# A short convolution and a SwiGLU block on one core: the copy that holds back the first weight transfers, and the order of the work of the first two pairs

## The chip, the core and the metric

The kernel runs on one core of one Trainium2 chip. The core has five engines with a queue of instructions each: TensorE (PE; its weight loads are listed as PEld), VectorE (DVE), ScalarE (ACT), GpSimd (POOL) and SyncE (SP), which here only issues DMAs. Each engine works through its queue in order; between engines, semaphores say when something is ready. The metric is device microseconds (us) from one launch.

## What is computed

```python
w = softmax(weight)                      # 8 heads x 7 taps
x_pad = concat(zeros(B, 6, D), x)        # x: 8 x 4096 x 192, fp32
att[b, s, h, :] = sum_k w[h, k] * x_pad[b, s + k, h, :]      # heads of 24 columns
x = att.reshape(32768, 192)
xn = x / sqrt(mean(x * x) + 1e-6) * rms_g
g, val = xn @ w_gate, xn @ w_val         # 192 -> 1536
out = (g * sigmoid(g) * val) @ w_out     # 1536 -> 192
```

The three weight matrices of the second half arrive as 64-bit floats. The kernel reads each as two 32-bit words and puts a 32-bit float together from them ("conversion"). All arithmetic is in fp32 or in a split of fp32 into three parts that TensorE multiplies at its faster fp32r rate.

## The kernel before

**Pairs.** The 32,768 tokens go in 32 pairs of 512-token halves, 1,024 tokens a pair. Pair 0 is computed plainly (`plain`, L1099 to L1117, then `outer` for the output matmuls). Pair 1 multiplies fp32 operands (L890), in a Strassen-like scheme for the output (the steps `o1` to `o7`, L945, with sums of operands `h1` to `h4` made at L972). From pair 2 on, the input products run on split operands in fp32r (L918) with weights that were split during pair 1, written to DRAM (`wd`, L781) and read back through a ring of ten slots (`ring_load`, L798). Meanwhile the convolution, the norm and the split of the next pair are prepared on DVE, ACT and POOL.

**The order is written by hand.** Scheduling is manual. Pair 0's work between the engines is the string `START` and then the list `LATER`, whose letters each advance one generator: `s` silu on ACT (L1110), `v` the product with the value on DVE (L1117), `n` the norm of pair 1, `t` its way to DRAM, and `o` and `O` the conversions of the even and the odd blocks of `w_out`. A conversion of an output block takes three steps: two integer operations on DVE (L305, L313); five on ACT (L320, L321, L324, L325, L328); then one on DVE (L330) and two on POOL (L336, L337), the last of which writes 2 of the 12 row blocks of `wo_sb`. The last block that pair 0's output matmuls need is the sixth.

For pair 1 the words of `FIRST` are run in order, each placing instructions at the tail of the queues: `pN` advances TensorE's line by N steps; `Aga.1` is ACT's silu of cell a of block 1 (L995) and `Vma.1` DVE's product (L1002), which also frees the PSUM bank of that cell for a later matmul; `Vh3.5` is one operand sum on DVE (L972); `W` is one step of the weights' splitting (DVE L765, ACT L769, DVE L771, POOL L775, ACT L777, SP L781, in that order for each of ten splits); `Gmul+` is POOL's scaling of pair 2's norm (L503); `Spl`, `Sft` and `Sld` are DMAs (pair 2's tokens away and back, and pair 3's eight head loads); `An.0+` ACT's rounding of the first split operand (L683), `Gl.0+` POOL's difference (L826), `Vd.0+` DVE's (L828), `Vl.4+` DVE's (L826); `Acv0++` is ACT's first tap of pair 3's convolution (L449); `R` starts the ring.

**The first convolution.** Pair 0's convolution (`conv_first`, L391) is shared between two engines: DVE takes taps 1, 3, 5 and 6 over eight heads into `y` (first tap L420, the others L424), ACT takes taps 0, 2 and 4 head by head (L406), and TensorE adds up ACT's products in PSUM with a unit matrix (L410), four heads a group. Of ACT's last tap, `give` heads are left to DVE (L430). Then DVE adds the two sums (L436). TensorE's `heat` matmuls (L536) run ahead of it.

**The hold.** Tokens of pair 0 are loaded first, in six DMAs: the first part of each partition's rows and then the second. The weights' DMAs stand behind them on SP. To keep them from competing with the tokens, `hold` copies three elements per partition from the tokens' last rows into the tile that the first weights are to be loaded to:

```python
def hold(t):
    nc.scalar.copy(out=t, in_=x0[:, -t.shape[1] :, 0])        # L226
```

The first weight DMA (L238) writes the same place and so waits for the copy, and the copy waits for the second part of the tokens. The copy is ACT's first instruction of the convolution; ACT's L406 stands behind it.

Of the kernel before, what the change touches and what calls it, by code (L numbers as in the profile page):

```python
# [20 lines left out]
def kernel(  # L21
# [10 lines left out]
    nc = tc.nc  # L32
# [61 lines left out]
    )  # L94
    FIRST = (
# [14 lines left out]
    )  # L110
    LINE = (
# [111 lines left out]

    def hold(t):

        nc.scalar.copy(out=t, in_=x0[:, -t.shape[1] :, 0])  # L226

    def load_in(u, q):
        cols = slice(u * NF * P, (u + 1) * NF * P)
# [27 lines left out]
    def load_out(i):  # L257


        if i < 2:  # L260
            t = outs.tile([P, T // P, D], F32, name="o_sb")
            t = t[:].rearrange("p j d -> p (j d)")
        else:
            n = PF * D * 2
            t = room[i // 2 - 1][:, (i % 2) * n : (i % 2 + 1) * n]
        t = raw["out", i] = t.bitcast(U32).rearrange("p (f d two) -> p f d two", f=PF, two=2)
        for f in range(PF):
            r = (i * PF + f) * P
            nc.sync.dma_start(out=t[:, f], in_=words(moe_w_out)[r : r + P, :, :])
# [117 lines left out]

    ys = {}

    def conv_first(mine, share, give):  # L390

        t = x_sb.pop(0)
        y = ys[0] = yp.tile([P, NJ, D], F32, name="y")
        theirs = [k for k in range(K) if k not in mine]
        two = NJ // 4
        for i, k in enumerate([theirs[0], mine[-1]] + theirs[1:]):
            xk, m = t[:, k : k + NJ, :], next(kept)
            if k in mine and not share:
                continue
            cuts = (0, share) if k in mine else (0, H // 2, H)  # L400
            if k == theirs[-1]:
                cuts = (0, H // 2, H - give)
            for lo, hi in zip(cuts, cuts[1:]):
                for h in range(lo, hi):
                    hs = slice(h * GS, (h + 1) * GS)
                    nc.scalar.mul(m[:, :, hs], xk[:, :, hs], taps[:, h, k : k + 1])  # L406
                part = slice(lo * GS, hi * GS)
                for c in range(4):
                    to = ps[c][:, 0 : two * D].rearrange("p (j d) -> p j d", d=D)
                    nc.tensor.matmul(  # L410
                        out=to[:, :, part], lhsT=unity, rhs=m[:, c * two : (c + 1) * two, part],
                        start=(i == 0 and lo == 0), stop=True, skip_group_check=True,
                    )
        for k in mine:
            xk = t[:, k : k + NJ, :]
            for h in range(share if k == mine[-1] else 0, H):
                hs = slice(h * GS, (h + 1) * GS)
                w = taps[:, h, k : k + 1]
                if k == mine[0]:
                    nc.vector.tensor_scalar(  # L420
                        out=y[:, :, hs], in0=xk[:, :, hs], scalar1=w, scalar2=None, op0=ALU.mult
                    )
                else:
                    nc.vector.scalar_tensor_tensor(  # L424
                        out=y[:, :, hs], in0=xk[:, :, hs], scalar=w, in1=y[:, :, hs],
                        op0=ALU.mult, op1=ALU.add,
                    )
        for h in range(H - give, H):
            k, hs = theirs[-1], slice(h * GS, (h + 1) * GS)
            nc.vector.scalar_tensor_tensor(  # L430
                out=y[:, :, hs], in0=t[:, k : k + NJ, hs], scalar=taps[:, h, k : k + 1],
                in1=y[:, :, hs], op0=ALU.mult, op1=ALU.add,
            )
        for c in (0, 3, 1, 2):
            at = y[:, c * two : (c + 1) * two, :].rearrange("p j d -> p (j d)")
            nc.vector.tensor_tensor(out=at, in0=ps[c][:, 0 : two * D], in1=at, op=ALU.add)  # L436
            if c % 2:
                heat(at, c)
# [723 lines left out]
    def done(it):  # L1162
# [11 lines left out]
        "ipvsicpsivpisvivcpsocvpispvscipvsipsiOvpsivipsvvpsopsvcpsvOnovoOpsonvOpsnoOvnopso"  # L1174
    )
    LATER = (
        (30, "s"), (35, "v"), (45, "v"), (47, "O"), (50, "O"), (53, "O"), (55, "n"), (60, "t"),
    )
    heat(taps[:].rearrange("p h k -> p (h k)"), 1)
    heat(unity, 14)  # L1180
# [7 lines left out]
        in1=mask[:].rearrange("p (o h) -> p o h", o=1).to_broadcast([P, K, H]), op=ALU.mult,  # L1188
    )
    nc.vector.tensor_reduce(out=tp[:], in_=own[:], axis=AX.X, op=ALU.add)  # L1190
    load_in(0, nc.sync)
    load_out(0)
    load_out(1)
    load_in(1, nc.sync)
    conv_first((1, 3, 5, 6), 0, 2)
    nc.gpsimd.memset(zeros, 0.0)
    nc.sync.dma_start(out=rg_sb[LOW, :], in_=rg)
    nc.sync.dma_start(out=rg_sb[UPP, 0 : KP - 1], in_=rg[:, 1:KP])
# [107 lines left out]
```

## Time and profile before

| | |
|---|---|
| time, median of 3 runs | 2470.25 us (2469.66 to 2471.25) |
| the profiled execution's own time | 2473.39 us |
| its span, first to last instruction | 2471.6 us |
| TensorE busy | 2452.5 us (99%) |
| VectorE busy | 2024.1 us (82%) |
| ScalarE busy | 1016.2 us (41%) |
| GpSimd busy | 833.3 us (34%) |
| granted TensorE clock | 1.0 |

A row of the timeline reads: start and duration in us, engine, line of the kernel, operation, output tile and inputs, shape, how many instructions were merged; in brackets the idle time of the engine ahead of it and what ended it. `SPq` is a DMA's issue. A row of the waits reads: engine, tile and line that waited, who was waited for, then total us, times and longest us. Ends of matmuls are modelled, so TensorE's idle time is less exact than its starts.

### The profile page before, as it was taken

What the parts mean: (1) busy time and instruction counts of PE and PEld (TensorE: products, weight loads), DVE (VectorE), ACT (ScalarE), POOL (GpSimd) and SP (SyncE); (2) the same over time, 40 slices, a digit from 0 to 9 for tenths busy, and PEclk for the clock granted to TensorE, in tenths of its full rate; (3) what the DMA queues carried; (4) which work ended last, traced back from release to release, by engine and by line L of the source; (5) the groups of instructions that cost most, each with busy time, mean ns of one, the idle gap of its engine ahead of it and who ended that gap; (6) DMA issues with size and microseconds to landing.
All of it is one profiled execution on the core that took longest, in us unless ns stands there. A gap on an engine that the chain in (4) does not pass through costs nothing.

```text
span 2471.6 us, 69198 instructions
## 1 busy us (share of the span) xinstructions
PE 2452.5 (99%) x29136; PEld 1894.3 (77%) x29136; DVE 2024.1 (82%) x2530; ACT 1016.2 (41%) x1431; POOL 833.3 (34%) x624
## 2 busy tenths in 40 slices
PE   8999999999999999999999999999999999999999
PEld 5547778887777777877777778777787787777777
DVE  8688888889888789888888787888888888888864
ACT  6443434433344434344334344333444343443332
POOL 0541343423343323334333434233433333333322
PEclk9999999999999999999999999999999999999999
DMA  7364678666677666786667776666776666876653
GB/s 152 60 207 125 175 184 211 179 171 170 164 200 195 181 165 172 176 207 181 190 158 178 179 202 186 176 168 168 199 197 187 165 172 169 203 192 188 159 161 95
DMA packets 716392, 430.55 MB, mean 174 GB/s; under 512 B 510330, under 2 KB 702386, under 8 KB 716082
## 3 DMA queue, kind: packets, MB, share of 16 engines
q1 hardware_dynamic: 712336, 425.21, 66.5%
q8 instruction: 230, 3.77, 0.7%
q10 hardware_dynamic: 3746, 0.92, 0.2%
q14 instruction: 80, 0.66, 0.1%
HBM read 366.96 MB, written 58.98 MB: 172 GB/s over the span
## 4 chain that ended last, share of the span: by engine, by line
PE 90%; DVE 3%; DMA 3%; SPq 1%; issue 1%; POOL 1%; ACT 1%; DVEq 0%; POOLq 0%; ACTq 0%
PE ps L918 55%; PE ps L945 35%; DMA xb<-xd 1%; DMA ht<-in_moe_w_val_dram 1%; DMA ring<-wd 1%; SPq L154 0%; DVE ht L972 0%; POOL part L775 0%; SPq L238 0%; DVE ht L1117 0%; DVE ht L1002 0%; DVE part L771 0%; DVE y L453 0%; DMA x<-in_x_dram 0%; DVE ps L989 0%
## 5 line engine op out<-in xcount | busy, mean ns | idle before, releaser
L918 PE MATMUL ps<-part,ring 64*128 64x512 f32 x12240 | 1422.0, 389 | 2.6 <-DMA ring<-wd 1.9
L918 PEld LDWEIGHTS ps<-part,ring 64*128 64x128 f32 x12240 | 1152.9, 184 | 257.8 <-DVE ps L989 12.5
L995 ACT ACTIVATE tt<-ps 128x512 f32<-128x512 f32 x744 | 438.9, 599 | 715.8 <-PE ps L918 661.7
L1002 DVE TENSOR_TENSOR ht<-ps,tt 128x512 f32<-128x512 f32 x744 | 498.0, 686 | 254.3 <-ACT tt L995 252.2
L945 PE MATMUL ps<-ht,wo_sb 128*32 128x384 f32 (+2 forms) x7272 | 468.3, 380 | 0.8 <-POOL wo_sb L337 0.8
L972 POOL TENSOR_TENSOR ht<-ht 128x512 f32<-128x512 f32 x180 | 272.2, 1520 | 543.9 <-PE ps L945 536.4
L945 PE MATMUL ps<-ht,x 128*32 128x256 f32 (+2 forms) x6696 | 439.1, 379 | 1.3 <-DVE ht L972 1.3
L945 PEld LDWEIGHTS ps<-ht,wo_sb 128*32 128x32 f32 x7272 | 325.1, 110 | 114.5 <-issue 14.5
L945 PEld LDWEIGHTS ps<-ht,x 128*32 128x32 f32 x6696 | 299.6, 110 | 90.9 <-DVE ht L972 1.6
L989 DVE TENSOR_TENSOR ps<-ps,tt 128x1024 f32<-128x1024 f32 x240 | 295.8, 1233 | 54.3 <-ACT tt L683 22.8
L453 DVE SCALAR_TENSOR_TENSOR y<-xh,tp,y 128x1536 f32<-128x1536 f32 x186 | 336.6, 1810 | 0.2
L683 ACT COPY ps<-ps 128x1024 f32<-128x1024 f32 (+1 forms) x151 | 134.6, 891 | 408.0 <-PE ps L918 336.5
L972 POOL TENSOR_TENSOR hs<-ht 128x512 f32<-128x512 f32 x120 | 155.0, 1292 | 262.6 <-DVE ht L1002 262.6
L683 ACT COPY tt<-ps 128x384 f32<-128x384 f32 (+1 forms) x182 | 151.7, 833 | 218.6 <-PE ps L945 154.9
L482 POOL TENSOR_SCALAR r<-r 128x8 f32<-128x8 f32 x31 | 6.1, 197 | 504.5 <-DVE r L477 504.4
L945 PE MATMUL ps<-hs,x 128*32 128x128 f32 (+2 forms) x2232 | 161.4, 379 | 0.0
L972 DVE TENSOR_TENSOR ht<-ht 128x512 f32<-128x512 f32 x192 | 135.0, 717 | 15.2 <-PE ps L945 12.6
L945 PEld LDWEIGHTS ps<-hs,x 128*32 128x32 f32 x2232 | 106.9, 110 | 29.6
L828 DVE SCALAR_TENSOR_TENSOR part<-part,xb 128x1024 fp32r<-128x1024 f32 x87 | 120.1, 1381 | 0.0
L972 DVE TENSOR_TENSOR ht<-hs,ht 128x512 f32<-128x512 f32 x156 | 109.2, 747 | 11.3 <-PE ps L945 10.7
L826 POOL TENSOR_TENSOR part<-xb,part 128x1024 fp32r<-128x1024 f32 x29 | 69.7, 2403 | 124.0 <-PE ps L918 82.1
L503 POOL TENSOR_TENSOR xh<-y,s 128x1536 f32<-128x1536 f32 x30 | 89.9, 2995 | 15.1 <-DVE s L495 8.6
(133 smaller groups left out, 1417.6 us busy)
## 6 DMA issues: line engine op xcount, KB each, us to landing
ring<-wd SPq DMA_DIRECT2D x1440, 192.0 KB
xb<-xd SPq DMA_DIRECT2D x60, 512.0 KB
xd<-xh SPq DMA_DIRECT2D x240, 96.0 KB
xh<-in_x_dram SPq DMA_DIRECT2D x192, 105.0 KB
xb<-xd SPq DMA_DIRECT2D x60, 256.0 KB
out_dram<-o_sb SPq DMA_DIRECT2D x126, 96.0 KB
out_dram<-o_sb SPq DMA_DIRECT2D x62, 128.0 KB
wd<-part SPq DMA_DIRECT2D x5, 1152.0 KB
```

The lines of the kernel that those rows point to most:

```text
L453: nc.vector.scalar_tensor_tensor(out=y, in0=xk, scalar=w, in1=y, op0=ALU.mult, op1=ALU.add)
L482: nc.gpsimd.tensor_scalar(out=r, in0=r, scalar1=s / D, scalar2=s * 1e-6, op0=ALU.mult, op1=ALU.add)
L503: e.tensor_tensor(out=yn[p].rearrange("p a t -> p t a"), in0=y, in1=ss[:].rearrange("p (t o) -> p t o", o=1).to_broadcast([P, TB, GS]), op ...
L683: nc.scalar.copy(out=dst, in_=src)
L826: e.tensor_tensor(out=split_of(g, 1).bitcast(F32R), in0=src, in1=high, op=ALU.subtract)
L828: nc.vector.scalar_tensor_tensor(out=split_of(g, 2).bitcast(F32R), in0=high, scalar=1.0 + SPLIT, in1=src, op0=ALU.mult, op1=ALU.subtract,)
L918: nc.tensor.matmul(out=self.both(j, c)[:, h, :], lhsT=left[HALF[h]], rhs=right[HALF[h]], start=(first and q == 0), stop=True, skip_group_c ...
L945: nc.tensor.matmul(out=self.acc(b)[i * Q : (i + 1) * Q, at : at + n], lhsT=left, rhs=cols, start=fresh, stop=True, skip_group_check=True, ...
L972: engine[eng].tensor_tensor(out=dst, in0=a, in1=b, op=op)
L989: nc.vector.tensor_tensor(out=self.both(j, c), in0=self.both(j, "b"), in1=s5, op=ALU.add)
L995: nc.scalar.activation(out=tt[:, t, :], in_=self.both(j, c)[:, 0, :], func=AF.Silu)
L1002: nc.vector.tensor_tensor(out=self.hv(j, "abcd".index(c)), in0=self.both(j, c)[:, 1, :], in1=tt[:, t, :], op=ALU.mult,)
```

## The change

Three things. The copy of `hold` goes from ACT to DVE; the function that issues the first weights' DMAs is called inside `conv_first`, so that the copy stands in DVE's queue behind the eight heads of its first tap. One more head of ACT's last tap stays with ACT: `give` goes from 2 to 1 and the last group has three heads instead of two. And words are moved: in `LATER` the three steps of the sixth output block's conversion come earlier; in `FIRST` one `W` and then three more go behind the products of cells a and b of pair 1's block 1, and `Acv0++` and the last DMAs of pair 3's tokens go ahead of `An.0+ An.4+ Gl.0+ Vd.0+ Vl.4+`.

```diff
 def hold(t):
-        nc.scalar.copy(out=t, in_=x0[:, -t.shape[1] :, 0])
+        nc.vector.tensor_copy(out=t, in_=x0[:, -t.shape[1] :, 0])
...
-    def conv_first(mine, share, give):
+    def conv_first(mine, share, give, then):
...
-                cuts = (0, H // 2, H - give)
+                cuts = (0, H // 2, H - give) if give else (0, H // 2, H // 2 + 2, H)
...
         for k in mine:
+            if k == mine[1]:
+                then()
...
     LATER = (
-        (30, "s"), (35, "v"), (45, "v"), (47, "O"), (50, "O"), (53, "O"), (55, "n"), (60, "t"),
+        (30, "s"), (33, "O"), (35, "v"), (37, "O"), (44, "O"), (45, "v"), (55, "n"), (60, "t"),
     )
...
-    load_in(0, nc.sync)
-    load_out(0)
-    load_out(1)
-    load_in(1, nc.sync)
-    conv_first((1, 3, 5, 6), 0, 2)
+
+    def first_loads():
+        load_in(0, nc.sync)
+        load_out(0)
+        load_out(1)
+        load_in(1, nc.sync)
+
+    conv_first((1, 3, 5, 6), 0, 1, first_loads)
...
     FIRST = (
-        "Vmc.0 W p1 Gpow+ W W W p1 W p1 Agd.0 W p1 Vmd.0 Vbc+ Vh1.0 p1 Gmul+ p1 Vh3.0 W",
-        "p1 Aga.1 W W W Vma.1 Vh2.0 p1 W W p1 Spl.0+ p1 Agb.1 Vmb.1 Spl.1+ p1 Spl.2+ W p1 Spl.3+ W",
+        "Vmc.0 W p1 Gpow+ W W W p1 W p1 Agd.0 W p1 Vmd.0 Vbc+ Vh1.0 p1 Gmul+ p1 Vh3.0",
+        "p1 Aga.1 Vma.1 p3 Agb.1 Vmb.1 W W W W Vh2.0 W W Spl.0+ Spl.1+ p1 Spl.2+ W p1 Spl.3+ W",
...
-        "p1 Vmd.5 p1 Vh1.5 p2 Ac1 Sld.3++ Vh3.5 Vh2.5 An.0+ An.4+ Gl.0+ Vd.0+ Vl.4+ p3 Sld.4++",
-        "Sld.5++ Sld.6++ Sld.7++ p1 Vh4.5 p1 Vh4.0 R Acv0++ p1 As7 p4 p2 Ac2 p1 Vcv1++ Vcv2++ Vh4.3",
+        "p1 Vmd.5 p1 Vh1.5 p2 Ac1 Sld.3++ Vh3.5 Vh2.5 Sld.4++ Sld.5++ Sld.6++",
+        "Sld.7++ Acv0++ An.0+ An.4+ Gl.0+ Vd.0+ Vl.4+ p4 Vh4.5 p1 Vh4.0 R p1 As7 p4 p2 Ac2 p1 Vcv1++ Vcv2++ Vh4.3",
```

Built, the queues differ only so. On SP, POOL and TensorE the instructions and their order are the same (TensorE's last group of L410 has 72 columns a row pair instead of 48). On DVE, the copy stands between L420 and L424 and one L430 is gone; L305 and L313 of the sixth block stand ahead of the last two L1117, and its L330 ahead of the last of them; one L765 stands behind two L1002 instead of ahead of them. On ACT, the copy is gone and one L406 is added; two L995 stand ahead of an L777 and an L769 instead of behind and between them; L449 stands ahead of two L683.

## Prediction

> **What bounds the kernel now.** I read the span by stretches first, then TensorE's waits, before and behind the microsecond at which pair 2's fp32r products begin.
>
> ```profile
> span 2471.6 us, 69198 instructions
> ...
> 31.00:97.40 66.40, 66.23 (x396) 31.67 (x396) 60.06 (x88) 42.97 (x68) 15.45 (x16) 1.00 0.37 75
> 214.03:2471.60 2257.57, 2249.26 (x27434) 1779.73 (x27432) 1850.76 (x2268) 917.34 (x1252) 767.00 (x562) 1.00 0.69 178
> ...
> PE ps L918 <- DMA ring<-wd: 1.9, 5, 0.8
> ```
>
> A row of the stretches gives its length, then busy time (and number of instructions) of TensorE, its weight loads, DVE, ACT and POOL, the granted clock, the share of the DMA engines and GB/s. Behind 214 us TensorE is busy for 2249.26 of 2257.57 us at a granted clock of 1.00, and the only wait its list shows there is for the ring. No instruction of that stretch is touched. So the change can only bring its beginning forward or push it back: by what TensorE waits for in the first 214 us, and by the time at which its work starts at all. From 31 to 97.4 us TensorE is as good as full (66.23 of 66.40), so what is left is the beginning and the three waits that the steps show. Nothing here can gain more than those few microseconds of 2471.6; that is the frame of all that follows. About 0.2% (4.9 us) is what a measurement of this kernel can tell from no change.
>
> **Step 1, the hold and the shared taps.**
>
> ```profile
> 5.03 5.30 PE L536 MATMUL ps<-part 128*128 128x128 f32 x28
> 7.48 1.92 DVE L420 TENSOR_SCALAR y<-x,taps 128x192 f32<-128x192 f32 x8 [2.21 <-DMA x<-in_x_dram]
> 8.94 0.20 ACT L226 COPY ht<-x 128x3 f32<-128x3 f32 x1 [5.43 <-DMA x<-in_x_dram]
> 9.11 7.71 ACT L406 ACTIVATE part<-x,taps 128x192 f32<-128x192 f32 x22
> 9.16 1.87 SPq L238 DMA_DIRECT2D ht<-in_moe_w_gate_dram  x3
> 9.32 7.98 DVE L424 SCALAR_TENSOR_TENSOR y<-x,taps,y 128x192 f32<-128x192 f32 x24
> 10.66 7.96 PE L410 MATMUL ps<-part 128*128 128x192 f32 x48 [0.33 <-ACT part L406]
> 17.22 0.74 DVE L430 SCALAR_TENSOR_TENSOR y<-x,taps,y 128x192 f32<-128x192 f32 x2
> 18.07 2.08 DVE L436 TENSOR_TENSOR y<-ps,y 128x384 f32<-128x384 f32 x4
> ```
>
> DVE could start at 7.48, with the first part of the tokens; ACT could have too, but its copy waited for the second part until 8.94, and 22 head-taps stood behind it. Without it ACT starts some 1.6 us earlier and does 23 in 23 x 0.35 (7.71/22) = 8.1 us: done by 15.6. TensorE's groups then wait for the heat matmuls, which end at 10.33, and run on without gaps: 48 rows took 7.96 us, paced by ACT; the last group grows by half, so 8.2 us at that pace, and the end comes no later than 18.5 instead of 18.62. Rows inside a group follow each other faster than groups do, so I expect about 18.2.
>
> DVE does what sets the end. Its copy goes between 9.32 and the 24 taps. The trace has no such copy on DVE; the bounds are its smallest single steps, L430's own pace less nothing (0.37 for a whole tap) above and nothing below, and I take ACT's 0.20 for the same three elements. One L430 goes: 0.37. So L436 starts at 18.07 - 0.11 (it waited that long for TensorE after L430's end at 17.96) - 0.37 + 0.20, about 17.8. Its second addition started when TensorE was through, and is the one to gain most: **0.3 to 0.4 us, I take 0.35**, bounds 0 (TensorE still ends at 18.6) and 0.5. What follows to 31 us is a chain of DVE, ACT and TensorE steps and moves along, and from there TensorE is full.
>
> The weights' DMAs now wait for DVE: from 9.16 to about 9.5, **0.35 us later**. Their queue is full, so each lands that much later.
>
> ```profile
> 12.36 4.62 DMA ht<-in_moe_w_val_dram
> ...
> 23.60 0.42 DVE L305 TENSOR_SCALAR part<-ht 128x384 uint32<-128x384 uint32 x1
> ```
>
> The last of the first block lands at 16.98 and is first read at 23.60: 6.6 us of slack, where the change uses 0.7 (0.35 late, 0.35 asked earlier). That is what hides it. Later blocks come through the same queue, 0.35 later each, and are converted by a DVE that is busy for 60.06 of the 66.40 us, in the stretch in which TensorE lacks nothing. Cost: 0; if that cover were gone, 0.35, which is the whole gain of this step.
>
> **Step 2, the sixth output block.**
>
> ```profile
> 90.86 6.71 PE L945 MATMUL ps<-ht,wo_sb 128*32 128x384 f32 x120
> 91.24 1.06 ACT L1110 ACTIVATE tt<-ps 128x512 f32<-128x512 f32 x2
> 91.85 1.29 DVE L1117 TENSOR_TENSOR ht<-ps,tt 128x512 f32<-128x512 f32 x2 [0.52 <-ACT tt L1110]
> 93.06 0.35 DVE L305 TENSOR_SCALAR part<-hs 128x384 uint32<-128x384 uint32 x1
> ...
> 95.59 0.58 ACT L328 ACTIVATE hs<-hs 128x384 f32<-128x384 uint32 x1
> ...
> 97.34 0.99 POOL L337 TENSOR_TENSOR wo_sb<-part 128x384 f32<-128x384 f32 x1
> 98.38 24.91 PE L945 MATMUL ps<-ht,wo_sb 128*32 128x384 f32 x456 [0.81 <-POOL wo_sb L337]
> ```
>
> TensorE's 120 rows for ten row blocks went out from 90.86; at the pace of the next 456 rows (24.91/456) they take 6.56, so the eleventh block was due at 97.42 and started at 98.38: 0.96 lost, a little more than the 0.8 of idle, whose ends are modelled. It waited for L337 (to 98.33), which follows ACT's L328, which follows, four ACT steps back, DVE's L305 at 93.06; and ACT was free at 92.30 (91.24 + 1.06). With L305 ahead of the two L1117, ACT need not wait: it starts 1.1 us earlier, at 92.3 instead of 93.4, if L305 and L313 are done by then. ACT needs L313 only two steps later, so a little delay there is covered. L337 then ends near 97.2. **I take 0.95**, bounds 0.5 and 1.0. The two L1117 pay: the last stands behind L330, which follows L328's end (95.59 + 0.58 - 1.1 = 95.1); with 0.35 for it, as for L305, and half of 1.29 it ends near 96.1 instead of 93.14. It feeds the third of four output cells; a cell is 144 rows, 7.8 us, so that one starts at 106: covered by some 10 us.
>
> **Step 3, two products ahead of the splitting.**
>
> ```profile
> 139.42 3.31 POOL L503 TENSOR_TENSOR xh<-y,s 128x1536 f32<-128x1536 f32 x1
> 139.93 3.08 DVE L765 TENSOR_SCALAR part<-part 128x512 uint32<-128x512 uint32 x1
> 140.24 0.58 ACT L995 ACTIVATE tt<-ps 128x512 f32<-128x512 f32 x1
> 142.93 0.67 DVE L1002 TENSOR_TENSOR ht<-ps,tt 128x512 f32<-128x512 f32 x1
> 143.66 2.85 PE L890 MATMUL ps<-xb,part 64*128 64x512 f32 x12 [1.15 <-DVE ht L1002]
> 144.12 0.68 DVE L771 SCALAR_TENSOR_TENSOR part<-part 128x512 f32<-128x512 f32 x1
> 144.88 1.27 POOL L775 TENSOR_TENSOR part<-part 128x512 f32<-128x512 f32 x1 [2.15 <-DVE part L771]
> ...
> L1002 DVE TENSOR_TENSOR ht<-ps,tt 128x512 f32<-128x512 f32 x24 | 16.2, 682 | 3.6 <-ACT tt L995 3.6
> ...
> 155.48 2.85 PE L890 MATMUL ps<-xb,part 64*128 64x512 f32 x12 [0.26 <-DVE ht L1002]
> ```
>
> TensorE stood at 143.66 for a bank that L1002 frees; L1002 stood behind an L765 that took 3.08 us, against 0.68 for L771 on a tile of the same shape. It ended 0.3 us after POOL's L503 (139.42 + 3.31 = 142.73): the two exclude each other. Now the silu of cell a follows its matmul instead of an L777, both L1002 run in 139.9 to 141.3, while L765 could not have moved. They read PSUM, and the 24 of them in this stretch average 682 ns, so that not one can have been held as long as that L765. So TensorE does not wait here: 1.2 us. But it does not keep them. Its next banks come out of the loop L771, L775, L777, L769, and L771 moves only by the L1002 that no longer stands between it and L765: 0.67. POOL's L775 follows it, unless the next L765, now free to go a little ahead of it, excludes POOL for its own time, as much as L771's 0.68: then nothing is left. TensorE runs into that loop again at the latest at 155.48, where it already waited (0.26). Between nothing and 0.67 **I take 0.3**; bounds -0.6 (the loop comes one L1002 later instead, since L777 now stands behind two L995 of 0.58 each) and 1.45 (TensorE keeps all of both waits).
>
> **Step 4, ACT's first tap ahead of two roundings.**
>
> ```profile
> 194.85 1.05 ACT L683 CAST part<-ring 128x1024 fp32r<-128x1024 f32 x1
> 195.97 2.37 POOL L826 TENSOR_TENSOR part<-ring,part 128x1024 fp32r<-128x1024 f32 x1 [11.27 <-ACT part L683]
> 196.01 2.88 DVE L972 TENSOR_TENSOR ht<-ht 128x512 f32<-128x512 f32 x1
> 196.12 1.51 PE L945 MATMUL ps<-ht,wo_sb 128*32 128x384 f32 x24
> 196.74 1.58 ACT L449 ACTIVATE y<-xh,tp 128x1536 f32<-128x1536 f32 x1
> 198.95 4.76 PE L945 MATMUL ps<-ht,x 128*32 128x384 f32 x84 [1.31 <-DVE ht L972]
> 199.00 0.69 DVE L972 TENSOR_TENSOR ht<-hs,ht 128x512 f32<-128x512 f32 x1
> 199.61 1.22 DVE L828 SCALAR_TENSOR_TENSOR part<-part,ring 128x1024 fp32r<-128x1024 f32 x1
> ```
>
> TensorE's 1.3 us are the L972 that takes 2.88 instead of 0.69: POOL's L826, released by the rounding that ended at 195.90, started 0.04 earlier. With L449 (1.58) ahead of that rounding, L826 comes at 197.5; both remaining L972 are through by 197.4 (196.01 + 2 x 0.69), and TensorE goes on at 196.12 + 24 x 0.0546 = 197.43. **1.45 us**, bounds 1.15 (TensorE goes on as late as 197.7, when L826 would delay the last L972 by what is left of it) and 1.5. L449 needs pair 3's tokens 1.9 us sooner than now; it did not wait for them. The price is in L828 and the L826 behind it, which now meet POOL's L826.
>
> The Trainium skill, SBUF, section "Who interferes with whom", says that a DVE instruction with two SBUF inputs and a GpSimd instruction that reads SBUF lock each other out for a whole instruction, whoever starts first. The 2.88 above agrees. By it DVE's differences would wait out POOL's for up to 2.4; the sum would stay, since the split's first reader is the product at 214.
>
> **Sum.** 0.35 + 0.95 + 0.3 + 1.45 = 3.05 us. The profiled execution took 2473.39, 3.1 above the median of the runs shown, so it would come to 2470.3, and the median from 2470.25 to **2467.2 us**.
>
> **The rivals.**
> - *TensorE keeps everything.* The loop of step 3 yields before TensorE gets there: 0.5 + 1.0 + 1.45 + 1.5 = 4.45, time 2465.8. For it: of the banks that come out of the loop behind 143.66, only the one at 155.48 was late, and by 0.26. Against it: L771's own shift is 0.67 only.
> - *The waits only change their name.* In two places the change doesn't do what it says: L436 stays behind TensorE (0), the loop comes 0.6 later; 0 + 0.95 - 0.6 + 1.45 = 1.8, time 2468.4. For it: L777's delay.
> - *The ring falls otherwise.* The 30 pairs behind 214 us lose 1.9 in five waits for the ring, 0.38 each. The transfers are not touched, but beside the same DMAs of the tokens they begin at another moment. If each of the 30 pairs lost as much, that were 30 x 0.38 - 1.9 = 9.5 more, less 3.05 is 6.4, time 2476.7: **slower**; it decides from eight further waits (8 x 0.38 = 3.04). If the five went as well, all kept, 4.45 + 1.9 = 6.35, time 2463.9. Against both: three runs within 1.6 us of each other.
>
> **How the numbers follow.** Forecast 0.50, everything kept 0.23, changed names 0.13, ring better 0.08, ring worse 0.06. The range takes in the bounds' sums, 4.45 and 1.05 (0 + 0.5 - 0.6 + 1.15, step 4 as low as a start at 197.7), and the 1.0 by which the runs lie apart from their median: 2464.8 to 2470.2. The two ring cases, 0.14, and little else lie outside. Faster than 2465.3 (0.2%): the better ring and half of "everything kept", 0.20. Slower than 2475.2: most of the worse one, 0.05. Within: 0.75.
>
> **What would show it.** Step 1: L406 starts at 7.5 and the weights' L238 at 9.5; L436 near 17.8. Step 2: L945 goes through 456 and 120 rows without the wait for `wo_sb`. Step 3: no wait at cell d of block 1, a longer one than 0.26 at 155.48 less the shift. Step 4: L972 near 0.69, no wait for it. In all, the first L918 near 211 instead of 214.03. I would be wrong if that comes at 214, or if it comes at 211 and the span does not follow.

## The result and the profile after

Before 2469.77 us (median of 15 runs, 2468.64 to 2472.17), after 2465.93 us (15 runs, 2464.3 to 2469.59): 3.84 us less, ratio 0.9984, 95% interval 0.9976 to 0.9992. The forecast was 2467.2 us, 3.05 below the 2470.25 shown then. The profiled execution of the changed kernel has a span of 2464.8 us. From L416 on, lines are numbered two higher in the changed kernel: L436 is L438, L536 is L538, L890 is L892, L918 is L920, L945 is L947, L972 is L974, L1002 is L1004.

TensorE's waits in the first 214 us, then the stretch behind the first fp32r product and its waits, of the changed kernel (engine, tile and line, who was waited for: total us, times, longest; the columns of the stretch are those of the prediction):

```profile
PE ps L892 <- DVE ht L1004: 1.1, 2, 0.9
PE ps L538 <- DVE y L438: 0.7, 1, 0.7
...
211.32:2464.80 2253.48, 2246.54 (x27434) 1776.81 (x27432) 1853.10 (x2268) 918.36 (x1252) 767.54 (x562) 1.00 0.69 179
...
PE ps L920 <- DMA ring<-wd: 0.7, 2, 0.5
```

The waits for L972 (1.3) and for `wo_sb` (0.8) are gone; the one for L1002, 1.4 before, is 1.1. The first fp32r product starts at 211.32 instead of 214.03, 2.7 earlier; near 211 was forecast. The rest of the profiled pair's difference, 2257.57 less 2253.48, lies in the untouched stretch: 1.2 of those 4.1 are waits for the ring (1.9 before, 0.7 after), and 2.7 are TensorE's own busy time, whose ends are modelled (2249.26 and 2246.54).

The timeline of the changed kernel, in the four places of the change:

```profile
5.03 6.14 PE L538 MATMUL ps<-part 128*128 128x128 f32 x28
...
6.98 8.12 ACT L406 ACTIVATE part<-x,taps 128x192 f32<-128x192 f32 x23 [3.48 <-DMA x<-in_x_dram]
8.74 0.17 DVE L226 COPY ht<-x 128x3 f32<-128x3 f32 x1
8.81 7.99 DVE L426 SCALAR_TENSOR_TENSOR y<-x,taps,y 128x192 f32<-128x192 f32 x24
8.94 1.86 SPq L238 DMA_DIRECT2D ht<-in_moe_w_gate_dram  x3
...
11.00 7.65 PE L410 MATMUL ps<-part 128*128 128x192 f32 x48
...
16.84 0.42 DVE L432 SCALAR_TENSOR_TENSOR y<-x,taps,y 128x192 f32<-128x192 f32 x1
...
17.95 0.56 DVE L438 TENSOR_TENSOR y<-ps,y 128x384 f32<-128x384 f32 x1 [0.70 <-PE ps L410]
...
19.30 2.85 PE L538 MATMUL ps<-y,part 128*128 128x384 f32 x8 [0.65 <-DVE y L438]
...
90.92 31.45 PE L947 MATMUL ps<-ht,wo_sb 128*32 128x384 f32 x576
91.32 1.16 DVE L305 TENSOR_SCALAR part<-hs 128x384 uint32<-128x384 uint32 x1
...
92.40 1.18 DVE L313 TENSOR_SCALAR part<-hs 128x384 uint32<-128x384 uint32 x1
...
92.52 0.62 ACT L320 ACTIVATE part<-part,edge 128x384 uint32<-128x384 uint32 x1
...
96.41 1.01 POOL L337 TENSOR_TENSOR wo_sb<-part 128x384 f32<-128x384 f32 x1
...
139.01 1.38 DVE L1004 TENSOR_TENSOR ht<-ps,tt 128x512 f32<-128x512 f32 x2
140.30 1.84 DVE L767 TENSOR_SCALAR part<-part 128x512 uint32<-128x512 uint32 x1
...
147.99 5.42 PE L892 MATMUL ps<-xb,part 64*128 64x512 f32 x24 [0.26 <-DVE ht L1004]
154.28 2.85 PE L892 MATMUL ps<-xb,part 64*128 64x512 f32 x12 [0.87 <-DVE ht L1004]
...
194.82 0.69 DVE L974 TENSOR_TENSOR ht<-ht 128x512 f32<-128x512 f32 x1
...
196.22 4.77 PE L947 MATMUL ps<-ht,x 128*32 128x384 f32 x84
196.22 1.22 DVE L830 SCALAR_TENSOR_TENSOR part<-part,ring 128x1024 fp32r<-128x1024 f32 x1
196.25 3.43 POOL L828 TENSOR_TENSOR part<-ring,part 128x1024 fp32r<-128x1024 f32 x1 [12.75 <-ACT part L685]
197.36 3.40 DVE L828 TENSOR_TENSOR part<-tt,part 128x1024 fp32r<-128x1024 f32 x1
...
211.32 1.65 PE L920 MATMUL ps<-part,ring 64*128 64x512 f32 x12
```

Set beside the rows of before, instruction by instruction, TensorE is level at 19.30 (before 19.27), 0.92 ahead behind the eleventh row block, 2.24 ahead at 141.42 (the cell that waited until 143.66), 1.91 at 147.99, 1.20 at 154.28, and 2.73 at 196.22. So in this pair of profiles step 1 gave nothing, step 2 0.92, step 3 1.32 of which 1.04 was given back by 154.28, step 4 1.53.

### The profile page after: what moved, and what is told of

Its sections match the earlier page's. It is cut to its first block, busy times and chain, and to the rows that moved or that the text cites. A ratio compares the mean times of both kernels' runs of the same rounds, so it can differ in the third digit from the quotient of the medians.

```text
span 2464.8 us, 69197 instructions
## 1 busy us (share of the span) xinstructions
PE 2449.7 (99%) x29136; PEld 1892.1 (77%) x29136; DVE 2025.1 (82%) x2530; ACT 1017.7 (41%) x1431; POOL 835.0 (34%) x624
## 4 chain that ended last, share of the span: by engine, by line
PE 95%; DMA 2%; DVE 1%; SPq 1%; ACT 0%; issue 0%; POOL 0%; DVEq 0%; ACTq 0%
PE ps L920 56%; PE ps L947 36%; PE ps L1101 2%; PE ps L892 1%; DMA xb<-xd 1%; DMA ht<-in_moe_w_val_dram 0%; SPq L154 0%; DVE ht L1004 0%; DMA ring<-wd 0%; DMA x<-in_x_dram 0%; DVE ht L974 0%; SPq L238 0%; DVE part L773 0%; DMA ht<-in_moe_w_gate_dram 0%; DVE ps L991 0%
## 5 line engine op out<-in xcount | busy, mean ns | idle before, releaser
L920 PE MATMUL ps<-part,ring 64*128 64x512 f32 x12240 | 1419.3, 389 | 1.2 <-DMA ring<-wd 0.7
L920 PEld LDWEIGHTS ps<-part,ring 64*128 64x128 f32 x12240 | 1150.1, 184 | 256.7 <-issue 12.3
L997 ACT ACTIVATE tt<-ps 128x512 f32<-128x512 f32 x744 | 440.1, 600 | 716.7 <-PE ps L920 654.8
L1004 DVE TENSOR_TENSOR ht<-ps,tt 128x512 f32<-128x512 f32 x744 | 498.4, 687 | 250.7 <-ACT tt L997 248.6
L947 PE MATMUL ps<-ht,wo_sb 128*32 128x384 f32 (+2 forms) x7272 | 468.3, 380 | 0.0
L974 POOL TENSOR_TENSOR ht<-ht 128x512 f32<-128x512 f32 x180 | 271.7, 1516 | 545.5 <-PE ps L947 538.1
L947 PE MATMUL ps<-ht,x 128*32 128x256 f32 (+2 forms) x6696 | 439.3, 379 | 0.0
L947 PEld LDWEIGHTS ps<-ht,wo_sb 128*32 128x32 f32 x7272 | 325.1, 110 | 113.5 <-issue 14.8
L947 PEld LDWEIGHTS ps<-ht,x 128*32 128x32 f32 x6696 | 299.6, 110 | 89.6 <-issue 0.8
L974 POOL TENSOR_TENSOR hs<-ht 128x512 f32<-128x512 f32 x120 | 155.3, 1295 | 261.9 <-DVE ht L1004 261.9
L947 PE MATMUL ps<-hs,x 128*32 128x128 f32 (+2 forms) x2232 | 161.5, 379 | 0.0
L974 DVE TENSOR_TENSOR ht<-ht 128x512 f32<-128x512 f32 x192 | 133.1, 707 | 13.7 <-PE ps L947 9.7
L947 PEld LDWEIGHTS ps<-hs,x 128*32 128x32 f32 x2232 | 106.9, 110 | 29.6
L974 DVE TENSOR_TENSOR ht<-hs,ht 128x512 f32<-128x512 f32 x156 | 108.1, 741 | 12.3 <-PE ps L947 11.7
L828 POOL TENSOR_TENSOR part<-xb,part 128x1024 fp32r<-128x1024 f32 x29 | 69.9, 2409 | 121.8 <-PE ps L920 98.9
```

The lines of the kernel that those rows point to most:

```text
L828: e.tensor_tensor(out=split_of(g, 1).bitcast(F32R), in0=src, in1=high, op=ALU.subtract)
L920: nc.tensor.matmul(out=self.both(j, c)[:, h, :], lhsT=left[HALF[h]], rhs=right[HALF[h]], start=(first and q == 0), stop=True, skip_group_c ...
L947: nc.tensor.matmul(out=self.acc(b)[i * Q : (i + 1) * Q, at : at + n], lhsT=left, rhs=cols, start=fresh, stop=True, skip_group_check=True, ...
L974: engine[eng].tensor_tensor(out=dst, in0=a, in1=b, op=op)
L997: nc.scalar.activation(out=tt[:, t, :], in_=self.both(j, c)[:, 0, :], func=AF.Silu)
L1004: nc.vector.tensor_tensor(out=self.hv(j, "abcd".index(c)), in0=self.both(j, c)[:, 1, :], in1=tt[:, t, :], op=ALU.mult,)
```

## The experiments

Two distances are read from each trace: from the span's start to the matmuls on `y` (L536; the row of the kernel before follows), and from there to the first fp32r product (214.03 - 19.27 = 194.76).

```profile
19.27 2.85 PE L536 MATMUL ps<-y,part 128*128 128x384 f32 x8 [0.65 <-DVE y L436]
```

The second takes out what the beginning does by chance. "Fast" is the start of the first of TensorE's row matmuls that is followed after 0.11 us (heat) or 0.16 (L410), where the ones before it took 0.21 or 0.32. The kernels with a p and a number are the four steps alone and p4_pool; the seven from p4_pool to v_both in the table ran once each, so only their traces are read.

| kernel | heat ends | fast from | L410 | matmuls on y | from there to fp32r | first fp32r | profiled span |
|---|---|---|---|---|---|---|---|
| before | 10.33 | 9.16 | 10.66 to 18.62 | 19.27 | 194.76 | 214.03 | 2471.6 |
| after | 11.17 | 10.89 | 11.00 to 18.65 | 19.30 | 192.02 | 211.32 | 2464.8 |
| p1_hold | 11.02 | 10.64 | 10.86 to 18.51 | 19.16 | 194.84 | 213.99 | 2467.1 |
| p2_block | 10.28 | 8.89 | 10.25 to 18.21 | 18.86 | 193.88 | 212.74 | 2466.5 |
| p3_words | 11.05 | 10.67 | 10.89 to 18.42 | 19.07 | 194.53 | 213.60 | 2471.8 |
| p4_tap | 10.41 | 9.35 | 10.52 to 18.48 | 19.13 | 193.28 | 212.41 | 2464.7 |
| p4_pool | 9.80 | 8.07 | 10.12 to 18.09 | 18.74 | 194.81 | 213.55 | 2468.8 |
| b_less | 8.78 | 14.29 | 10.32 to 19.87 | 20.52 | 194.80 | 215.33 | 2468.3 |
| h_less | 8.77 | 10.80 | 8.57 to 17.31 | 18.44 | 191.96 | 210.40 | 2463.9 |
| h_four | 7.06 | 13.19 | 8.58 to 18.56 | 19.21 | 191.96 | 211.17 | 2464.2 |
| h_more | 11.53 | 8.91 | 11.37 to 19.01 | 19.66 | 191.97 | 211.63 | 2465.6 |
| v_first | 10.75 | 10.03 | 10.59 to 18.23 | 18.88 | 191.99 | 210.87 | 2464.8 |
| v_both | 9.96 | 8.35 | 9.80 to 17.45 | 18.51 | 190.74 | 209.24 | 2463.6 |
| best | 8.70 | 9.11 | 8.85 to 16.93 | 18.75 | 190.74 | 209.49 | 2463.4 |

The second distance repeats to 0.08 us in kernels that share its order (194.76 to 194.84; 191.96 to 192.02). It is the finest measure here: the medians of ten runs have intervals of some 2 us to each side.

### Each step alone, on the kernel before

```diff
-        nc.scalar.copy(out=t, in_=x0[:, -t.shape[1] :, 0])
+        nc.vector.tensor_copy(out=t, in_=x0[:, -t.shape[1] :, 0])
...
-                cuts = (0, H // 2, H - give)
+                cuts = (0, H // 2, H - give) if give else (0, H // 2, H // 2 + 2, H)
...
-    conv_first((1, 3, 5, 6), 0, 2)
+    conv_first((1, 3, 5, 6), 0, 1, first_loads)
```

> Step 1 alone on the kernel before (the copy on VectorE, one more head on ScalarE). Theory A: the end of the first convolution is set by TensorE, whose heat matmuls have to run their course at the rate that it has then; ScalarE's earlier start only moves the wait, so the matmuls behind the convolution start at 19.2 to 19.35 (19.27 before, 19.30 after), the first fp32r product of pair 2 at 213.9 to 214.1, and the median stays within 0.5 us of before. Rival B (the prediction): the heat matmuls of the changed kernel were late by chance (they turned fast at 10.9 instead of 9.2); where they turn fast at 9.2 the products behind the convolution start near 18.9, the first fp32r product at 213.7. Rival C: step 1 also pays behind 214 us, and most of the 3.9 us that the long stretch was shorter comes with it: the median falls by 1.5 us or more.

Measured: matmuls on `y` at 19.16, first fp32r product at 213.99, 2468.13 us beside 2469.47 (ratio 0.9997, 0.9987 to 1.0006). The trace says A, by 0.04 below its window at the matmuls on `y`; the median fell by 1.3 where A said at most 0.5, and C at least 1.5: the interval holds both, so time settles nothing here. The traces speak against C: behind the first fp32r product p1_hold's profile took 2253.1 us against 2257.5 before, but p2_block, p4_tap and b_less, without step 1, took 2252.3 to 2253.8. The heat turned fast at 10.64, late again, so this run alone can't show B; two kernels below, with the same first convolution (v_first, v_both), do.

```diff
-        (30, "s"), (35, "v"), (45, "v"), (47, "O"), (50, "O"), (53, "O"), (55, "n"), (60, "t"),
+        (30, "s"), (33, "O"), (35, "v"), (37, "O"), (44, "O"), (45, "v"), (55, "n"), (60, "t"),
```

> Step 2 alone on the kernel before (the sixth output block's conversion earlier). Theory A: TensorE's wait for wo_sb at 98.4 goes whole, and all that lies behind it comes 0.9 to 0.95 earlier up to the waits of pair 1, where some of it may be lost: L945 goes on at 97.45, the first fp32r product at 213.1 to 213.4. Rival B: the DVE products that now stand behind the conversion come to bind, and the next cell starts with a wait: the gain is under 0.6.

Measured: no wait for `wo_sb`, and the second distance is 0.88 shorter; 2467.29 us (ratio 0.9993, 0.9984 to 1.0002). A. That the first fp32r product came at 212.74, ahead of A's window, is a first convolution that ended 0.41 earlier than in the profile of before, though nothing of it was touched: ScalarE's L406 started at 8.70 instead of 9.11, since the tokens came earlier.

```diff
-        "Vmc.0 W p1 Gpow+ W W W p1 W p1 Agd.0 W p1 Vmd.0 Vbc+ Vh1.0 p1 Gmul+ p1 Vh3.0 W",
-        "p1 Aga.1 W W W Vma.1 Vh2.0 p1 W W p1 Spl.0+ p1 Agb.1 Vmb.1 Spl.1+ p1 Spl.2+ W p1 Spl.3+ W",
+        "Vmc.0 W p1 Gpow+ W W W p1 W p1 Agd.0 W p1 Vmd.0 Vbc+ Vh1.0 p1 Gmul+ p1 Vh3.0",
+        "p1 Aga.1 Vma.1 p3 Agb.1 Vmb.1 W W W W Vh2.0 W W Spl.0+ Spl.1+ p1 Spl.2+ W p1 Spl.3+ W",
```

> Step 3 alone on the kernel before (two L1002 ahead of the splitting). Theory A: the wait of 1.15 at 143.66 goes, but the splitting loop and the L1002 behind it come only about 0.3 earlier, so waits of about 0.25 near 149.9 and 0.9 near 155.5 take its place, and the first fp32r product starts 0.2 to 0.4 earlier than 214.03. Rival B: TensorE keeps 1.2 or more: the first fp32r product at 212.9 or before. Rival C: the loop comes later, and it is no gain or a loss: 214.0 to 214.6.

Measured: 0.24 shorter, waits of 0.27 and 0.86 in place of 1.15 and 0.26; 2469.29 us (ratio 0.9998, 0.9988 to 1.0007). A. (The first fp32r product, at 213.60, is 0.43 earlier, of which 0.20 come from the beginning.)

```diff
-        "p1 Vmd.5 p1 Vh1.5 p2 Ac1 Sld.3++ Vh3.5 Vh2.5 An.0+ An.4+ Gl.0+ Vd.0+ Vl.4+ p3 Sld.4++",
-        "Sld.5++ Sld.6++ Sld.7++ p1 Vh4.5 p1 Vh4.0 R Acv0++ p1 As7 p4 p2 Ac2 p1 Vcv1++ Vcv2++ Vh4.3",
+        "p1 Vmd.5 p1 Vh1.5 p2 Ac1 Sld.3++ Vh3.5 Vh2.5 Sld.4++ Sld.5++ Sld.6++",
+        "Sld.7++ Acv0++ An.0+ An.4+ Gl.0+ Vd.0+ Vl.4+ p4 Vh4.5 p1 Vh4.0 R p1 As7 p4 p2 Ac2 p1 Vcv1++ Vcv2++ Vh4.3",
```

> Step 4 alone on the kernel before (ScalarE's first tap ahead of two roundings). Theory A: L972 takes 0.69 instead of 2.88, TensorE's wait of 1.3 at 198.95 goes, and the first fp32r product starts 1.4 to 1.55 earlier, at 212.5 to 212.65. Rival B: the locked pair moves: the differences that VectorE now takes beside POOL's are late for the last sums (L972), which then hold TensorE between 199 and 214; the gain is under 1.0.

Measured: 1.48 shorter; 2467.41 us (ratio 0.9995, 0.9985 to 1.0004). A. (The product, at 212.41, is 0.09 ahead of A's window; the beginning was 0.14 earlier.) The four parts add up to -0.07 (0.07 longer) + 0.88 + 0.24 + 1.48 = 2.53 us, against 2.75 for all together (from 194.76 to 192.02): what the steps do to each other is some 0.2.

### Is it the heat that hid step 1?

The heat on the unit matrix, on the changed kernel with 8, 20 and 4 matmuls (h_less, h_more, h_four), and on the kernel before with 8 (b_less):

```diff
-    heat(unity, 14)
+    heat(unity, 8)
```

> The changed kernel with 8 heat matmuls on the unit matrix instead of 14. Theory A (TensorE's heat holds up the first convolution, and so hid step 1): L410 starts at 8.5 to 8.8 instead of 11.0, as soon as ScalarE's first four head-taps are there (8.48); it ends by 17.2, VectorE becomes the bound (its last tap ended at 17.26), L438 starts near 17.3 without waits between its four, and the matmuls on y start near 18.45 instead of 19.30: 0.7 to 0.9 earlier, all of which reaches the first fp32r product (210.4 to 210.6 instead of 211.3). Rival B: the matmuls need the heat to turn fast; without it L410 runs at the slow rate, about twice as long a row, for long enough to end at 18.6 or later, and nothing is gained.

The timeline of this kernel:

```profile
8.57 8.74 PE L410 MATMUL ps<-part 128*128 128x192 f32 x48
18.44 1.88 PE L538 MATMUL ps<-y,part 128*128 128x384 f32 x5 [1.14 <-DVE y L438]
```

A, but for 0.1 at L410's end: L410 from 8.57 to 17.31, the matmuls on `y` at 18.44, the first fp32r product at 210.40. It was so although a quarter of L410 ran at the slow rate, up to 10.80.

> The changed kernel with 20 heat matmuls instead of 14. Theory A: six more matmuls at the fast rate (0.22 each) end the heat 1.3 later, L410 and all behind it move with them: the matmuls on y start near 20.6 instead of 19.30, the first fp32r product near 212.6. Rival B: VectorE or the tokens set the end of the convolution: the matmuls on y stay within 0.4 of 19.30.

The number is B's, 19.66, 0.36 later; the reason is A's. Six matmuls more at 0.22 are 1.33, but the heat ended only 0.36 later, because it turned fast at 8.91 here and at 10.89 in the profile of the changed kernel. The table gives the rule: with step 1 and 14 or 20 heat matmuls, L410 ends 7.48 after the heat, each time, but for rounding (18.65 - 11.17, 18.51 - 11.02, 19.01 - 11.53, and in two kernels further down 18.23 - 10.75 and 17.45 - 9.96). So the heat's end sets L410's, and the heat's end hangs on when it turns fast. The first theory B is right in that: in v_both, fast at 8.35, the matmuls on `y` start at 18.51. Without step 1 it is ScalarE's start, and so the tokens, that set L410's end: it comes 9.51 after the first L406 in the four profiles with 14 heat matmuls that ended by 10.41 (18.62 - 9.11, 18.21 - 8.70, 18.48 - 8.97, 18.09 - 8.58); only in p3_words, where the heat ended at 11.05, is it later (18.42 - 8.45 = 9.97).

> The kernel BEFORE with 8 heat matmuls instead of 14. Theory A (step 1 is worth something only where the heat doesn't stand in its way, and the short heat only with step 1): ScalarE still begins its taps behind the copy at 8.9 to 9.1, the first four are there at 10.6, so L410 starts at 10.4 to 10.7 as before and ends between 18.1 and 18.6; the matmuls on y start at 18.7 to 19.3, the first fp32r product at 213.5 to 214.1: no gain. Rival B (the short heat alone is the gain): the matmuls on y start by 18.5.

Neither: it lost 1.3 us. The timeline of this kernel:

```profile
5.04 3.74 PE L536 MATMUL ps<-part 128*128 128x128 f32 x16
8.78 7.71 ACT L406 ACTIVATE part<-x,taps 128x192 f32<-128x192 f32 x22
10.32 9.55 PE L410 MATMUL ps<-part 128*128 128x192 f32 x48 [1.54 <-ACT part L406]
...
19.24 2.16 DVE L436 TENSOR_TENSOR y<-ps,y 128x384 f32<-128x384 f32 x4 [1.59 <-PE ps L410]
```

L410 started at 10.32, just ahead of A's window, with ScalarE's four head-taps. But TensorE had stood still for 1.5 us before that, and L410 then ran at 0.32 us a row up to 14.29. In these profiles the short heat is a loss without step 1 and a gain of 0.86 with it.

> The changed kernel with 4 heat matmuls on the unit matrix. Theory A: the heat is over near 7, L410 starts when ScalarE's first four head-taps are there (8.5) and VectorE sets the end, as with 8: the matmuls on y within 0.3 of 18.45. Rival B: TensorE's idle stretch between 7 and 8.5 keeps it at the slow rate longer; rows of L410 at some 0.3 us in place of 0.16 go on past 11, it ends past 18, and the matmuls on y start at 18.8 or later.

B by its mechanism: with 1.51 idle ahead of L410 the rows took 0.32 up to 13.19, L410 ended at 18.56, the matmuls on `y` started at 19.21. The heat is there to have no pause, not to be short: 4 matmuls leave one of 1.5, 8 none or 0.15 (best, below), 14 are in the way.

How differently TensorE works in the same 4 us shows in the number of its instructions in the window from 9 to 13 us; first this kernel, then the one with 8:

```profile
9.00:13.00 4.00, 4.00 (x14) 4.00 (x14) 4.00 (x13) 4.00 (x13) 0.00 (x0) 1.00 0.67 160
```

```profile
9.00:13.00 4.00, 4.00 (x21) 4.00 (x21) 4.00 (x13) 4.00 (x13) 0.00 (x0) 1.00 0.67 159
```

14 and 21 instructions in a TensorE that is busy throughout, at a granted clock of 1.00 both times.

### What brings pair 1's waits back?

On the changed kernel, VectorE's product of cell a of block 2 ahead of one operand sum:

```diff
-        "p1 W W W p1 W Vh3.1 W Vh2.1 p1 Aga.2 Vma.2 p2 W p1 Agb.2 W W W Vmb.2 p1 W W p2 Agc.2",
+        "p1 W W W p1 W Vh3.1 W p1 Aga.2 Vma.2 Vh2.1 p2 W p1 Agb.2 W W W Vmb.2 p1 W W p2 Agc.2",
```

> The changed kernel with VectorE's product of cell a of block 2 (L1004) ahead of one operand sum (L974) that takes 1.56 beside POOL's L777. Theory A: the wait of 0.87 at 154.28 is that order on VectorE, since ScalarE's silu had been ready since 151.1: TensorE's wait goes or falls below 0.2, and the first fp32r product comes 0.6 to 0.9 earlier than 211.3. Rival B (the prediction's step 3): TensorE runs into the splitting loop again at once: the next banks are as late, a wait of 0.5 or more turns up at cells b or c, and the product comes less than 0.4 earlier.

The second distance stayed at 191.99: nothing was kept. (The product at 210.87 is 0.45 earlier, 0.42 of it by the beginning, 18.88 instead of 19.30.) The timeline of this kernel, first ScalarE and VectorE ahead of the second wait, then TensorE:

```profile
159.37 1.06 ACT L997 ACTIVATE tt<-ps 128x512 f32<-128x512 f32 x2
...
160.83 1.26 DVE L974 TENSOR_TENSOR hs<-ht 128x512 f32<-128x512 f32 x1
162.12 1.66 DVE L974 TENSOR_TENSOR ht<-ht 128x512 f32<-128x512 f32 x1
163.88 0.69 DVE L974 TENSOR_TENSOR ht<-hs,ht 128x512 f32<-128x512 f32 x1
164.49 0.68 DVE L1004 TENSOR_TENSOR ht<-ps,tt 128x512 f32<-128x512 f32 x1
...
147.54 8.00 PE L892 MATMUL ps<-xb,part 64*128 64x512 f32 x36 [0.25 <-DVE ht L1004]
165.23 2.85 PE L892 MATMUL ps<-xb,part 64*128 64x512 f32 x12 [0.98 <-DVE ht L1004]
```

The wait of 0.87 went and came back as 0.98 eleven microseconds later. It is B's outcome; whether by B's mechanism is another matter: the L1004 that ended this wait stood behind three L974, and the silu that it reads, the second L997, had been ready since 160.43. That looks like the same fault again, not like the loop; the next run asks.

With that edit and this one, cell a of block 3 ahead of two of three sums:

```diff
-        "Vmc.2 p1 W p1 W W W p1 Agd.2 W p1 Vmd.2 W Vh1.2 p2 Vh3.2 Vh2.2 p1 Aga.3 W Vma.3 p1 W",
+        "Vmc.2 p1 W p1 W W W p1 Agd.2 W p1 Vmd.2 W Vh1.2 p3 Aga.3 Vma.3 Vh3.2 Vh2.2 W p1 W",
```

> The changed kernel with two products ahead of operand sums: cell a of block 2 as in v_first, and cell a of block 3 (L1004, whose silu was ready 4 us before it) ahead of two of the three sums before it. Theory A (the waits of pair 1 come from the order on VectorE, one after the other, and each removed wait is kept but for what the next bank lacks): no wait near 165, one of about 0.2 near 170.5 (that bank had 0.79 to spare); from the matmuls on y to the first fp32r product it takes 191.0 to 191.4 instead of 192.0. Rival B (the splitting loop's own length sets the end of pair 1): a wait of 0.7 or more turns up behind 165, and the distance stays within 0.3 of 192.0.

TensorE's timeline of this kernel:

```profile
147.16 8.00 PE L892 MATMUL ps<-xb,part 64*128 64x512 f32 x36 [0.26 <-DVE ht L1004]
155.09 0.86 PE L947 MATMUL ps<-ht,wo_sb 128*32 128x384 f32 x12
155.88 10.57 PE L892 MATMUL ps<-xb,part 64*128 64x512 f32 x48
```

No wait is left behind 147.16, and the distance is 190.74: 1.25 less than with the first product alone, more than A had promised, because the bank that lacked 0.2 came in time. The splitting loop does not set the end of pair 1: what did was an L1004 behind operand sums, twice, and the second hid behind the first.

### Is step 4's gain a matter of POOL's start?

On the kernel before:

```diff
-        "p1 Vmd.5 p1 Vh1.5 p2 Ac1 Sld.3++ Vh3.5 Vh2.5 An.0+ An.4+ Gl.0+ Vd.0+ Vl.4+ p3 Sld.4++",
-        "Sld.5++ Sld.6++ Sld.7++ p1 Vh4.5 p1 Vh4.0 R Acv0++ p1 As7 p4 p2 Ac2 p1 Vcv1++ Vcv2++ Vh4.3",
+        "p1 Vmd.5 p1 Vh1.5 p2 Ac1 Sld.3++ Vh3.5 Vh2.5 An.0+ An.4+ p3 Sld.4++",
+        "Sld.5++ Sld.6++ Sld.7++ p1 Vh4.5 Gl.0+ Vd.0+ Vl.4+ p1 Vh4.0 R Acv0++ p1 As7 p4 p2 Ac2 p1 Vcv1++ Vcv2++ Vh4.3",
```

> The kernel before with ScalarE's order untouched (first tap L449 behind the two roundings); instead POOL's difference L826 and VectorE's two (L828, L826) are put behind the sum Vh4.5, so POOL's still starts when the first rounding is through (195.9) unless it waits for something of VectorE's. Theory A (what held L972 for 2.88 is POOL's L826 at the same time, not the order on VectorE): POOL still starts L826 near 196.0, L972 takes 2.9 again and TensorE waits 1.3 again; the first fp32r product stays near 214.0. Rival B (L972 waits because VectorE's own later work is in its way): L972 takes 0.69, the wait goes, and the product comes 1.4 earlier.

The timeline of this kernel, and then that of p4_tap:

```profile
195.49 2.37 POOL L826 TENSOR_TENSOR part<-ring,part 128x1024 fp32r<-128x1024 f32 x1 [11.27 <-ACT part L683]
195.53 2.88 DVE L972 TENSOR_TENSOR ht<-ht 128x512 f32<-128x512 f32 x1
...
198.46 3.89 PE L945 MATMUL ps<-ht,x 128*32 128x384 f32 x66 [1.31 <-DVE ht L972]
```

```profile
195.18 0.69 DVE L972 TENSOR_TENSOR hs<-ht 128x512 f32<-128x512 f32 x1
195.91 0.69 DVE L972 TENSOR_TENSOR ht<-ht 128x512 f32<-128x512 f32 x1
196.70 0.69 DVE L972 TENSOR_TENSOR ht<-hs,ht 128x512 f32<-128x512 f32 x1
197.34 3.42 POOL L826 TENSOR_TENSOR part<-ring,part 128x1024 fp32r<-128x1024 f32 x1 [12.75 <-ACT part L683]
```

A: VectorE's own differences stand elsewhere, POOL's difference starts where it did, 0.04 ahead of L972, and L972 takes the same 2.88. In p4_tap, where POOL starts at 197.34, three L972 in a row take 0.69 each. What decides is which of the two starts first.

### The three together

```diff
-    heat(unity, 14)
+    heat(unity, 8)
...
-        "p1 W W W p1 W Vh3.1 W Vh2.1 p1 Aga.2 Vma.2 p2 W p1 Agb.2 W W W Vmb.2 p1 W W p2 Agc.2",
+        "p1 W W W p1 W Vh3.1 W p1 Aga.2 Vma.2 Vh2.1 p2 W p1 Agb.2 W W W Vmb.2 p1 W W p2 Agc.2",
...
-        "Vmc.2 p1 W p1 W W W p1 Agd.2 W p1 Vmd.2 W Vh1.2 p2 Vh3.2 Vh2.2 p1 Aga.3 W Vma.3 p1 W",
+        "Vmc.2 p1 W p1 W W W p1 Agd.2 W p1 Vmd.2 W Vh1.2 p3 Aga.3 Vma.3 Vh3.2 Vh2.2 W p1 W",
```

> The changed kernel with 8 heat matmuls and both products earlier. If both theories A hold, the matmuls on y start near 18.45, the first fp32r product 191.0 to 191.4 behind them, at 209.5 to 209.9 (before 214.04, changed kernel 211.32), and the median comes 1.2 to 2.0 us below the changed kernel's 2465.93, ratio to the kernel before 0.9975 to 0.998. If waits only move, the ratio stays near 0.9984.

```profile
7.30 8.06 ACT L406 ACTIVATE part<-x,taps 128x192 f32<-128x192 f32 x23 [3.80 <-DMA x<-in_x_dram]
...
17.15 0.42 DVE L432 SCALAR_TENSOR_TENSOR y<-x,taps,y 128x192 f32<-128x192 f32 x1
```

Measured (the fence has two rows of its timeline): 209.49, 190.74 behind the matmuls on `y`; 2464.19 us (8 runs, 2462.95 to 2465.31) beside 2470.74, ratio 0.9974, interval 0.9963 to 0.9984. The matmuls on `y` came at 18.75, later than expected, since the tokens came later (L406 at 7.30, 6.98 in the changed kernel's profile) and VectorE's last tap ended at 17.57 (17.26): with a short heat the tokens set it. The interval overlaps with the changed kernel's (0.9976 to 0.9992), so by time alone it is not shown to be faster; by the trace its fp32r products start 1.8 us sooner.

## Why the prediction came out as it did

*The frame* held: TensorE gains only what it no longer waits for in the first 214 us. The trace shows 2.7 for a forecast of 3.05.

*Step 1* is the term that failed, 0 instead of 0.35. The instructions did as forecast, a little earlier since the tokens came earlier: L406 at 6.98, the weights' L238 at 8.94, VectorE's last tap over at 17.26, with one such tap fewer. The step that failed is "TensorE's groups then wait for the heat matmuls, which end at 10.33 ... Rows inside a group follow each other faster than groups do, so I expect about 18.2." The heat ended at 11.17 in the profile of the changed kernel, not at 10.33; L410 ended 7.48 behind it, at 18.65, and L438 waited 0.7 for it. The heat's end is not a constant: it fell between 9.80 and 11.17 in the nine kernels with 14 matmuls.

By the table the step is worth what that draw leaves: the matmuls on `y` started at 19.30, 19.16, 18.88 and 18.51 with it (mean 18.96), and at 19.27, 18.86, 19.07, 19.13 and 18.74 without (mean 19.01), 0.05 less, with draws that overlap. The draws with the step were later, too (the heat ended at 10.73 in the mean, against 10.37). Of two kernels whose heat ended alike, p1_hold with the step started them at 19.16 and p3_words without it at 19.07 (heat to 11.02 and 11.05), v_both at 18.51 and p4_pool at 18.74 (9.96 and 9.80). Had the heat of the changed kernel ended at 10.33, as the step assumed, L410 would have ended near 17.81 by the 7.48 above, and the matmuls on `y`, 0.65 behind it as in that profile, would have started near 18.5. With the tokens as late as in the profile of before, VectorE would have set the end: its last tap near 17.76 (17.96 - 0.37 + 0.17 for the copy) and the 1.18 that h_less takes from there to the matmuls on `y` (18.44 - 17.26) give 18.9, some 0.3 before 19.27. Both are estimates from these rows, not measurements. So the 0.35 was right for the heat's end that it took, and wrong to take that end as given. The bound of 0 named just this ("TensorE still ends at 18.6") and was nearer than the value taken. With 8 heat matmuls the changed kernel shows what the heat held back, 19.30 - 18.44 = 0.86. That the weights come no later than they are needed held; L238 was issued sooner than before.

*Step 2* held: 0.92 in the changed kernel, 0.88 alone, for 0.95. L305 now ran beside POOL's L337 and took 1.16 instead of 0.35 (L313, beside L336, took 1.18, and 1.17 before), so ACT began 0.2 later than forecast and L337 ended at 97.42 instead of 97.2; it was enough.

*Step 3* held in size and in its main reason, that the gain comes back as later waits: 0.28, and 0.24 alone, for 0.3. TensorE gained 1.32 at 141.42 and ran into later waits (0.26 and 0.87). What was wrong is the cause named for these: "Its next banks come out of the loop L771, L775, L777, L769". The one of 0.26 at 147.99 does; its L1004 stands behind an L773 that waited 2.56 for ScalarE's L771, and it is in each kernel that has step 3. The one of 0.87 doesn't: it came from an L1004 behind an operand sum that POOL's L777 had stretched to 1.57, and v_both shows that the loop leaves room for 1.25 more. The wait of 0.26 at 155.48 in the kernel before, which the prediction put down to the loop, was already this one: its L1002 started at 154.74, behind an L972 of 1.57, 2.4 us after its silu was through (152.31). The two rows, from the changed kernel's timeline:

```profile
146.37 0.96 DVE L773 SCALAR_TENSOR_TENSOR part<-part 128x768 f32<-128x768 f32 x1 [2.56 <-ACT part L771]
...
152.05 1.57 DVE L974 TENSOR_TENSOR ht<-hs,ht 128x512 f32<-128x512 f32 x1
```

*Step 4* held: 1.53, and 1.48 alone, for 1.45; p4_pool shows that POOL's start is the cause. The price named, "L828 and the L826 behind it, which now meet POOL's L826", came too: VectorE's took 3.40 instead of 1.22, nothing followed from it. The Trainium skill's rule (SBUF, "Who interferes with whom") agrees in both directions: the 3.40 ended at 200.76, 1.08 after POOL's 3.43 that had itself begun during a VectorE instruction of 1.22.

*The rivals.* "TensorE keeps everything" is out for steps 1 and 3. "The waits only change their name" had step 1 right and step 3 wrong. "The ring falls otherwise" is true of single executions: in the 14 profiles the ring costs between nothing (p4_tap) and 3.0 us (p3_words, in three waits), without an edit behind 214 us in either, and the profile of before, with 1.9, lay at the upper end.

```profile
PE ps L918 <- DMA ring<-wd: 3.0, 3, 1.5
```

So of the 6.8 us between the two profiled spans, 2.7 are the change. The medians say 3.84, with an interval from 2.0 to 5.9 (0.9992 and 0.9976 of 2469.77) that holds 2.7. Whether the untouched stretch has a share in the remaining 1.1 stays open: the profiles of a kernel are too few for it. From the first fp32r product to the end, the seven kernels that lack some of the steps took 2252.3 to 2258.2, and the seven that have all took 2253.0 to 2254.4, so the 2257.5 of before looks like a long draw. By the trace the forecast was 0.3 too high and by the medians 0.8 too low; that the median lies inside the range owes nothing to step 1.

## What to carry to other kernels

A wait removed from a pipeline is worth what the next bank has to spare: list the slack at each later hand-over before pricing it, and if the gain comes back as a wait, look at what that wait stands behind before blaming the loop, since it may be the same fault once more. A step that frees one engine is worth nothing while another sets the end; the engine to look at was the one that was only being kept warm. Measure changes of a microsecond by distances between two events within a trace, which repeat to 0.08 us here, not by medians.

## What was not expected of the hardware

TensorE began its dense work at 4.58 to 4.71 in the 14 profiles, and its matmuls doubled their rate (0.21 to 0.11 us apart, or 0.32 to 0.16) between 8.07 and 10.89 in the 12 kernels that gave it no pause of over 0.4: 3.47 to 6.30 us later, from one execution to the next. Where it paused for 1.5 us after 8.78 or 7.06, in one profile each, the change came at 14.29 and 13.19, 4.0 and 4.6 behind the restart. The granted clock in the profile is 1.00 on both sides of it.

The Trainium skill (TensorE: Matmul & The Clock Gate, part 1) tells of an activity window of about 3.4 us that runs free and must be busy as a whole. The 3.47 to 6.30 us agree with that: by this figure the first whole window ends between 3.4 and 6.8 us after the work begins (an estimate). The spread of 2.8 us does not agree with the 500 ns to each side that the same part of the Trainium skill gives for the change.
